# One pool of three 2 KB tiles for exponentials, key projections, copied key-value sums and output staging

## The chip, the cores and the metric

The kernel runs on one core of a Trainium2 chip. The metric is device time in microseconds (us) of one execution. Five engines work side by side, each through its own queue in a fixed order: TensorE (PE, matmuls; its weight loads are shown as PEld), VectorE (DVE), ScalarE (ACT), GpSimd (POOL) and SyncE (SP), which issues all DMAs here. They meet only at semaphores.

## The reference

Linear attention with random features, then a two-layer network on all tokens (8 batches, 8 heads, 576 tokens, head width 64, 128 features; 4608 tokens, model width 512, inner width 2048):

```python
def phi(x):
    proj = np.einsum('bhsd,df->bhsf', x, w_phi)
    proj = proj - np.max(np.abs(proj), axis=-1, keepdims=True)
    return np.concatenate([np.exp(proj), np.exp(-proj)], axis=-1)
q_p, k_p = phi(q), phi(k)
kv = np.einsum('bhsf,bhsd->bhfd', k_p, v)
z = np.sum(k_p, axis=2)
num = np.einsum('bhsf,bhfd->bhsd', q_p, kv)
den = np.einsum('bhsf,bhf->bhs', q_p, z)[..., None] + 1e-06
x = (num / den).transpose(0, 2, 1, 3).reshape(4608, 512)
h = x @ w_in
out = np.maximum(0.01 * h, h) @ w_out
```

## The kernel before

**Attention** goes by pairs of heads: 8 batches of 4 pairs, numbered 0 to 31. Pairs 0 to 3 have their own start-up code (`first_k_phase`, `first_q_phase`); pairs 4 to 31 use `k_phase` and `q_phase`. From pair 8 on, every fp32 operand is split in a high and a low fp32r half, and products are made of three matmuls (hh, hl, lh).

`k_phase(i)` walks the 576 keys in three groups (two columns of 128 tokens, two, one of 64). A group projects the keys on PE (L244), copies and adds the two halves into a tile `pmk` (128 x 512 fp32, which is 2 KB in a partition; L67 by `copy_`, L249), takes the largest magnitude (L252) and negates it (L256). Each column then is exponentiated with both signs into a tile `ek` (L269, L270), split into `kph` (ACT, L67) and `kpl` (POOL or DVE, L72), and multiplied with the values into the PSUM tile `kvp` (L224). At the end `kvp` is copied to SBUF (`kvs`), transposed on PE (L301) and split into `kvh` and `kvl` (L313, L314).

`q_phase(i)` projects the queries in two halves of 288 tokens and two heads: four PSUM tiles, each made by L344 and L345, turned on DVE (L346), with block maxima (L348). The maxima cross the partitions by DMA: three DMAs `m<-m` (L350), a reduction on DVE (L353), three DMAs `mx<-mx` (L355). Then for each half: subtraction (L361), transposition back (L363), two exponentials for each head (L368, L369), the split into `qh` (DVE, L375) and `ql` (POOL, L72), and the matmuls with the key-value sums (L384, L386, L389). The result is divided and written into `ring`, which holds two batches.

**The network** takes blocks of 256 tokens, 18 of them, in 16 steps each. A step makes 128 inner features (`layer1`: 12 matmuls, L571, L572, L574, into PSUM tile `h`), applies the activation (L578), splits it into `gh` (ACT) and `gl` (POOL), and three steps later `layer2` adds the step into two PSUM tiles `acc` of 128 tokens (6 matmuls, L591 to L593). After the 16th step each `acc` is copied to an SBUF tile `o` (L67 on ACT for one, L69 on DVE for the other) and stored (L599). There are two `acc` slots, so layer 2 of the next block begins when the two copies are made. Blocks 0 and 1 run together while the weights are loaded; block 1 accumulates in an `h` and an `a` slot of PSUM in place of `acc`.

**What sets the order.** The kernel is written in a framework whose scheduler plans every engine's queue before the run. It takes ready instructions by priority: attention has the lower number, which goes first, and the network fills what is left. `advance` and `room` keep attention at most a ring ahead. A tile is named by a tag, with a number of slots for each tag (`BUFS`, else one); a new tile takes a slot when the tile before it in that slot has been released, and an instruction that writes a new tile is planned only when it has a slot. On the chip the planned order of each queue is fixed.

In SBUF the tag `ek` has one slot (exponentials, `kvs`, the last output tile, and two of four start-up tiles), `pmk` one and `o` one, each of 2 KB in a partition.

Of the kernel before, what the change touches and what calls it, by code (L numbers as in the profile page):

```python
# [9 lines left out]
F32 = mybir.dt.float32  # L10
# [7 lines left out]
P = 128  # L18
B, H, S, D = 8, 8, 576, 64
NP = H // 2  # L20
F = 128
U = 288
DM = 512
# [5 lines left out]
NBLK = NTOK // T  # L29
LAG = 3  # L30
NN = 8
NK = 8
BUFS = {"kph": 2, "eq": 2, "m4": 2, "g": 2, "gh": 2, "gl": 2, "qh": 2, "ql": 2, "dn": 2}
PBUFS = {"a": 3, "c": 1, "h": 2, "acc": 2}
ENG = {"vh": "a", "kst": "v", "qh": "v", "o": "av", "kpl": "pppv", "ksub": "vvp", "l": "v"}
TINY = 2.0 ** -15
# [8 lines left out]
def attention_moe_kernel(ctx: ExitStack, tc: tile.TileContext, q, k, v, vt, w_phi, w_in, w_out, out):  # L45
    nc = tc.nc
    cp = ctx.enter_context(tc.tile_pool(name="cp", bufs=1))
    sp = ctx.enter_context(tc.tile_pool(name="sp", bufs=1))
# [2 lines left out]
    def ct(shape, dt, name):  # L51
        return cp.tile(shape, dt, tag=name, name=name)

    def st(shape, dt, tag):
        return sp.tile(shape, dt, tag=tag, name=tag, bufs=BUFS.get(tag, 1))

    cnt = {}

# [146 lines left out]
    def k_phase(i):  # L205
        nat = i < NK
        rk, rv = kraw.pop(i)
        if not nat:
            ks = st([P, 2, S], F32R, "ks")
            for j in range(2):  # L210
                o, n = slice(64 * j, 64 * j + 64), slice(64 - 64 * j, 128 - 64 * j)
# [15 lines left out]
        for g in range(3):  # L227
# [1 line left out]
            r = slice(0, P) if g < 2 else slice(64, P)  # L229
            n = P if g < 2 else 64  # L230
            m4 = st([P, 4], F32, "m4")
            pmk = st([P, 4, F], F32, "pmk")
            if nat:
                pk = pt("a")
                for s in range(w):
# [23 lines left out]
            yield  # L259
            for s in range(w):  # L260
                c = 2 * g + s
                ek = st([P, 2, 256], F32, ("ek", "kph", "kpl")[c % 3] if nat else "ek")
                if nat:
                    nc.scalar.activation(ek[r, :, 0:F], pmk[r, 2 * s : 2 * s + 2], AF.Exp)
                    nc.scalar.activation(ek[r, :, F:256], pmk[r, 2 * s : 2 * s + 2], AF.Exp, scale=-1.0)
                else:
                    for j in range(2):
                        h = 2 * s + j
                        nc.scalar.activation(ek[r, j, 0:F], pmk[r, h], AF.Exp, bias=m4n[r, h : h + 1])  # L269
                        nc.scalar.activation(ek[r, j, F:256], pmk[r, h], AF.Exp, scale=-1.0, bias=m4[r, h : h + 1])  # L270
                if nat:
                    for j in range(2):
                        kv_mm(j, rv[r, 4 * j + c if c < 4 else 8 + j], ek[r, j], first=c == 0, last=c == 4)
                    yield
                    continue
                if c < 4:
                    kph = st([P, 2, 256], F32R, "kph")
                    kpl = st([P, 2, 256], F32R, "kpl")
                    copy_("kph", kph, ek)
                    tt_("kpl", kpl, ek, kph.bitcast(F32), ALU.subtract)  # L280
                    for j in range(2):
                        kv_mm(j, vh[:, 4 * j + c], kph[:, j], first=c == 0)
                        kv_mm(j, vl[:, 4 * j + c], kph[:, j])
                    for j in range(2):
                        kv_mm(j, vh[:, 4 * j + c], kpl[:, j])
                else:
                    kst = st([P, 2, 256], F32R, "kph")
                    copy_("kst", kst[r], ek[r])
                    nc.vector.tensor_tensor(kst[0:64], ek[r], kst[r].bitcast(F32), op=ALU.subtract)
                    for j in range(2):  # L290
                        kv_mm(j, vl[:, 8 + j], kst[:, j])
                        kv_mm(j, vh[:, 8 + j], kst[:, j], last=True)
                yield
        kvs = st([P, 2, 256], F32, "ek").rearrange("p a (b f) -> p a b f", b=2)[0:66]
        copy_("kvs", kvs, kvp[0:66].rearrange("p (a b f) -> p a b f", a=2, b=2))
        yield
        kvt = pt("c")
# [113 lines left out]
    def first_k_phase(i):  # L411
        od = i % 2
        rk, rv = first_k.pop(i)
        if i == 2:
            load_k(NP)
        yield
        kvp = pt("h")
        for g in range(3):
            pk = pt("a" if od else "acc")
            w = 2 if g < 2 else 1  # L420
            for s in range(w):
                t0 = (2 * g + s) * P if g < 2 else S - P
                proj(pk, s, rk[:, t0 : t0 + P])
            r = slice(0, P) if g < 2 else slice(64, P)
            n = P if g < 2 else 64
            m4 = st([P, 4], F32, "m4")
            pkv = pk[r, 0 : 256 * w].rearrange("p (a f) -> p a f", f=F)
            nc.vector.tensor_reduce(m4[r, 0 : 2 * w], pkv, axis=AX.X, op=ALU.max, apply_absolute_value=True)
            pm = st([P, 4, F], F32, ("kpl" if g % 2 else "kph") if od else ("ek" if g % 2 else "pmk"))
            nc.vector.tensor_tensor(pm[r, 0 : 2 * w], pkv,  # L430
                                    m4[r, 0 : 2 * w].unsqueeze(2).broadcast_to([n, 2 * w, F]), op=ALU.subtract)
            yield
            first_k["e"] = ne = first_k.get("e", -1) + 1
            e = exps[ne % 3].rearrange("p (a t f) -> p a t f", t=2, f=F)
            nc.scalar.activation(e[r, 0 : 2 * w, 0], pm[r, 0 : 2 * w], AF.Exp)
            nc.scalar.activation(e[r, 0 : 2 * w, 1], pm[r, 0 : 2 * w], AF.Exp, scale=-1.0)
            for s in range(w):
                c = 2 * g + s
                for j in range(2):
                    nc.tensor.matmul(kvp[0:66, 256 * j : 256 * j + 256], lhsT=rv[r, 4 * j + c if c < 4 else 8 + j],  # L440
                                     rhs=e[r, 2 * s + j].rearrange("p t f -> p (t f)"),
                                     start=c == 0 and j == 0, stop=c == 4, skip_group_check=True)
                yield
        kvs = st([P, 2, 256], F32, "kph").rearrange("p a (b f) -> p a b f", b=2)[0:66]
        copy_("kvs", kvs, kvp[0:66].rearrange("p (a b f) -> p a b f", a=2, b=2))
        kvt = pt("c")
        kvtv = kvt[:, 0:264].rearrange("p (a b f) -> p a b f", a=2, b=2)
        for j in range(2):
            for t in range(2):
                nc.tensor.transpose(kvtv[:, j, t], kvs[:, j, t], ident[0:66, 0:66])  # L450
        kvh = first_kvh(i)
        nc.scalar.copy(kvh[:, :, :, 0:64], kvtv[:, :, :, 0:64])
        nc.scalar.copy(kvh[:, :, :, 64:P], kvtv[:, :, :, 64:65].broadcast_to([P, 2, 2, 64]))
        kvs_of[i] = kvh, None
        yield
# [17 lines left out]
    def first_q_phase(u):  # L473
# [7 lines left out]
        for hp in range(1 if tail else NP):  # L481
# [3 lines left out]
            m4 = st([P, 4], F32, "m4")  # L485
            pqv = pq[0:n, 0 : 256 * ns].rearrange("p (a f) -> p a f", f=F)
            nc.vector.tensor_reduce(m4[0:n, 0 : 2 * ns], pqv, axis=AX.X, op=ALU.max, apply_absolute_value=True)
            pm = st([P, 4, F], F32, "ek" if hp % 2 else "pmk")
            nc.vector.tensor_tensor(pm[0:n, 0 : 2 * ns], pqv,
                                    m4[0:n, 0 : 2 * ns].unsqueeze(2).broadcast_to([n, 2 * ns, F]), op=ALU.subtract)  # L490
            yield
# [91 lines left out]
    def layer2(i, ft, half=range(TT)):  # L583
# [9 lines left out]
            nc.tensor.matmul(a, lhsT=gl[:, ts], rhs=weight(1, "h", ft), start=False, stop=ft == NFT - 1)  # L593
        if ft == NFT - 1:
            for t in half:
                o = st([P, DM], F32, "ek" if i == NBLK - 1 and t else "o")
                copy_("o", o, accs[i, t])
                r = i * T + t * P
                nc.sync.dma_start(out[r : r + P, :], o)  # L599
# [88 lines left out]
```

## Time and profile before

| what | value |
|---|---|
| time, median of 3 runs (lowest, highest) | 1207.81 us (1206.63, 1209.95) |
| profiled execution: time, span from first to last instruction | 1207.22 us, 1205.4 us |
| granted TensorE clock, mean over the span | 0.992 |
| PE busy, share of the span | 1168.8 us, 97% |
| ACT, DVE, POOL busy | 861.8, 747.7, 631.5 us |
| last exponential of a key phase (L270) starts at | 1034.3 us |
| copies into `o`: ACT 18, DVE 17; first at | 222.9 us |

The span has three parts. To about 210 us pairs 0 to 7 run and the weights are loaded and split; from 210 to about 1060 us pairs 8 to 31 run among network steps; the rest is network alone. In the rows of the windows view, the columns are: stretch, its length, then busy time and instruction count of PE, PEld, DVE, ACT, POOL, the granted PE clock, the DMA share and GB/s. In the timeline view they are: start, length, engine, line, operation, output<-inputs, shapes, count, and in brackets the idle time of the engine just before, with what ended it. In the waits view: engine and line that waited, what for, total us, times, longest.

### The profile page before, as it was taken

What the parts mean: (1) busy time and instruction counts of PE and PEld (TensorE: products, weight loads), DVE (VectorE), ACT (ScalarE), POOL (GpSimd) and SP (SyncE); (2) the same over time, 40 slices, a digit from 0 to 9 for tenths busy, and PEclk for the clock granted to TensorE, in tenths of its full rate; (3) what the DMA queues carried; (4) which work ended last, traced back from release to release, by engine and by line L of the source; (5) the groups of instructions that cost most, each with busy time, mean ns of one, the idle gap of its engine ahead of it and who ended that gap; (6) DMA issues with size and microseconds to landing.
All of it is one profiled execution on the core that took longest, in us unless ns stands there. A gap on an engine that the chain in (4) does not pass through costs nothing.

```text
span 1205.4 us, 21633 instructions
## 1 busy us (share of the span) xinstructions
PE 1168.8 (97%) x7496; PEld 1035.9 (86%) x7496; DVE 747.7 (62%) x1327; ACT 861.8 (71%) x2267; POOL 631.5 (52%) x709
## 2 busy tenths in 40 slices
PE   8899999899998999899999999999999999999998
PEld 5577778699997999799998999899989999989997
DVE  5979984566767675766677666767876767510000
ACT  5977875778787787777787877778777788543232
POOL 0042222456566676666666666656566766453232
PEclk9999999899998999899999999999999999999999
DMA  7425241201111011111111011111011110000000
GB/s 215 142 81 167 88 116 32 77 23 33 50 32 48 18 44 33 50 24 32 50 32 40 22 50 33 40 33 50 21 40 32 41 33 19 3 18 5 14 18 18
DMA packets 70846, 57.82 MB, mean 48 GB/s; under 512 B 53201, under 2 KB 54353, under 8 KB 70737
## 3 DMA queue, kind: packets, MB, share of 16 engines
q1 hardware_dynamic: 70736, 56.44, 16.6%
q8 instruction: 59, 0.97, 0.3%
q14 instruction: 51, 0.41, 0.1%
HBM read 46.20 MB, written 9.44 MB: 46 GB/s over the span
## 4 chain that ended last, share of the span: by engine, by line
PE 69%; DVE 10%; ACT 9%; issue 4%; DMA 4%; SPq 2%; POOL 2%; DVEq 0%; POOLq 0%; ACTq 0%
PE h L571 9%; PE h L574 9%; PE h L572 9%; PE acc L591 8%; PE acc L592 8%; PE acc L593 8%; PE c L224 5%; PE a L384 2%; DMA mx<-mx 2%; PE a L244 2%; PE a L389 2%; PE a L386 2%; DMA m<-m 2%; DVE tq L361 1%; SPq L350 1%
## 5 line engine op out<-in xcount | busy, mean ns | idle before, releaser
L72 POOL TENSOR_TENSOR gl<-g,gh 128x256 fp32r<-128x256 f32 x288 | 231.3, 806 | 327.9 <-ACT gh L67 259.9
L571 PE MATMUL h<-xh,w0h 128*128 128x256 f32 x1088 | 281.1, 285 | 4.4 <-ACT g L578 2.4
L572 PE MATMUL h<-xh,w0l 128*128 128x256 f32 x1088 | 277.5, 282 | 0.0
L571 PEld LDWEIGHTS h<-xh,w0h 128*128 128x128 f32 x1088 | 205.9, 189 | 18.3 <-ACT g L578 4.2
L591 PE MATMUL acc<-w1h,gh 128*128 128x512 f32 x544 | 215.3, 396 | 0.7 <-DVE o L69 0.4
L592 PE MATMUL acc<-w1l,gh 128*128 128x512 f32 x544 | 214.8, 395 | 0.0
L572 PEld LDWEIGHTS h<-xh,w0l 128*128 128x128 f32 x1088 | 205.8, 189 | 8.9
L593 PE MATMUL acc<-w1h,gl 128*128 128x512 f32 x544 | 203.4, 395 | 0.7 <-POOL gl L72 0.7
L578 ACT ACTIVATE g<-h 128x256 f32<-128x256 f32 x288 | 109.1, 381 | 110.4 <-PE h L574 85.4
L574 PE MATMUL h<-xl,w0h 128*128 128x256 f32 x1088 | 187.4, 281 | 0.0
L72 POOL TENSOR_TENSOR ql<-eq,qh 128x576 fp32r<-128x576 f32 x96 | 148.8, 1569 | 53.6 <-DVE qh L375 31.7
L67 ACT CAST gh<-g 128x256 fp32r<-128x256 f32 x288 | 114.8, 403 | 57.5 <-PE acc L592 55.1
L574 PEld LDWEIGHTS h<-xl,w0h 128*128 128x128 f32 x1088 | 154.6, 188 | 0.6 <-POOL xl L72 0.2
L72 POOL TENSOR_TENSOR kpl<-ek,kph 128x512 fp32r<-128x512 f32 x72 | 98.4, 1366 | 37.4 <-ACT kph L67 14.5
L591 PEld LDWEIGHTS acc<-w1h,gh 128*128 128x128 f32 x544 | 102.4, 188 | 14.1 <-DVE o L69 0.7
L593 PEld LDWEIGHTS acc<-w1h,gl 128*128 128x128 f32 x544 | 99.1, 188 | 17.6 <-POOL gl L72 0.9
L592 PEld LDWEIGHTS acc<-w1l,gh 128*128 128x128 f32 x544 | 102.3, 188 | 12.6
L361 DVE TENSOR_TENSOR tq<-tq,mx 128x576 f32<-128x576 f32 x56 | 59.2, 1097 | 80.3 <-DMA mx<-mx 80.3
L269 ACT ACTIVATE ek<-pmk,m4n 128x128 f32<-128x128 f32 (+1 forms) x240 | 89.8, 393 | 16.1 <-POOL kpl L72 12.6
L375 DVE TENSOR_REDUCE qh<-eq 128x576 fp32r<-128x576 f32 x96 | 70.8, 749 | 44.4 <-ACT eq L369 20.2
L270 ACT ACTIVATE ek<-pmk,m 128x128 f32<-128x128 f32 (+1 forms) x240 | 89.1, 390 | 8.6 <-DVE m L252 8.1
L368 ACT ACTIVATE eq<-mb 128x288 f32<-128x288 f32 x112 | 49.2, 439 | 53.5 <-DVE mb L363 50.1
(202 smaller groups left out, 2363.9 us busy)
## 6 DMA issues: line engine op xcount, KB each, us to landing
out_dram<-o SPq DMA_DIRECT2D x35, 256.0 KB, 2.0
rq<-in_q_dram SPq DMA_DIRECT2D x28, 288.0 KB, 3.0
rk<-in_k_dram SPq DMA_DIRECT2D x27, 288.0 KB, 2.8
rv<-in_v_dram SPq DMA_DIRECT2D x29, 256.0 KB, 3.6
ring<-in_w_in_dram SPq DMA_DIRECT2D x9, 512.0 KB, 3.8
f<-in_w_out_dram SPq DMA_DIRECT2D x7, 512.0 KB, 3.6
f<-in_w_in_dram SPq DMA_DIRECT2D x7, 512.0 KB, 3.7
ring<-in_w_out_dram SPq DMA_DIRECT2D x5, 512.0 KB, 3.8
```

The lines of the kernel that those rows point to most:

```text
L67: nc.scalar.copy(o, i)
L72: (nc.vector if pick(key) == "v" else nc.gpsimd).tensor_tensor(o, a, b, op=op)
L269: nc.scalar.activation(ek[r, j, 0:F], pmk[r, h], AF.Exp, bias=m4n[r, h : h + 1])
L270: nc.scalar.activation(ek[r, j, F:256], pmk[r, h], AF.Exp, scale=-1.0, bias=m4[r, h : h + 1])
L361: nc.vector.tensor_tensor(tu, tu, mx[:, u].unsqueeze(2).broadcast_to([P, 18, 32]), op=ALU.subtract)
L571: nc.tensor.matmul(ph, lhsT=weight(0, "h", ft)[:, d * P : d * P + P], rhs=xh[d], start=d == 0, stop=False)
L572: nc.tensor.matmul(ph, lhsT=weight(0, "l", ft)[:, d * P : d * P + P], rhs=xh[d], start=False, stop=False)
L574: nc.tensor.matmul(ph, lhsT=weight(0, "h", ft)[:, d * P : d * P + P], rhs=xl[d], start=False, stop=d == NP - 1)
L578: nc.scalar.activation(g, ph, AF.Prelu, alpha=0.01)
L591: nc.tensor.matmul(a, lhsT=gh[:, ts], rhs=weight(1, "h", ft), start=ft == 0, stop=False)
L592: nc.tensor.matmul(a, lhsT=gh[:, ts], rhs=weight(1, "l", ft), start=False, stop=False)
L593: nc.tensor.matmul(a, lhsT=gl[:, ts], rhs=weight(1, "h", ft), start=False, stop=ft == NFT - 1)
```

## The change

Tags `ek`, `pmk` and `o` go; a tag `wk` with three slots of the same size takes their tiles, so the SBUF used is the same. `pmk` and `ek` of `k_phase`, `kvs`, all output tiles, and the start-up tiles that alternated between `ek` and `pmk` now draw from it. Tiles in `kph` and `kpl` stay where they were. No instruction is added, removed or resized.

```diff
-BUFS = {"kph": 2, "eq": 2, "m4": 2, "g": 2, "gh": 2, "gl": 2, "qh": 2, "ql": 2, "dn": 2}
+BUFS = {"kph": 2, "eq": 2, "m4": 2, "g": 2, "gh": 2, "gl": 2, "qh": 2, "ql": 2, "dn": 2, "wk": 3}
...
-    def st(shape, dt, tag):
-        return sp.tile(shape, dt, tag=tag, name=tag, bufs=BUFS.get(tag, 1))
+    def st(shape, dt, tag, name=None):
+        return sp.tile(shape, dt, tag=tag, name=name or tag, bufs=BUFS.get(tag, 1))
...
-            pmk = st([P, 4, F], F32, "pmk")
+            pmk = st([P, 4, F], F32, "wk", "pmk")
...
-                ek = st([P, 2, 256], F32, ("ek", "kph", "kpl")[c % 3] if nat else "ek")
+                ek = st([P, 2, 256], F32, ("wk", "kph", "kpl")[c % 3] if nat else "wk", "ek")
...
-        kvs = st([P, 2, 256], F32, "ek").rearrange("p a (b f) -> p a b f", b=2)[0:66]
+        kvs = st([P, 2, 256], F32, "wk", "kvs").rearrange("p a (b f) -> p a b f", b=2)[0:66]
...
-            pm = st([P, 4, F], F32, ("kpl" if g % 2 else "kph") if od else ("ek" if g % 2 else "pmk"))
+            pm = st([P, 4, F], F32, ("kpl" if g % 2 else "kph") if od else "wk", "pm")
...
-            pm = st([P, 4, F], F32, "ek" if hp % 2 else "pmk")
+            pm = st([P, 4, F], F32, "wk", "pm")
...
-                o = st([P, DM], F32, "ek" if i == NBLK - 1 and t else "o")
+                o = st([P, DM], F32, "wk", "o")
```

The scheduler plans again with these slots, and the queues change over their whole length. Three places matter for the prediction. A name's number is the tile's number in the program and is the same in both kernels.

**The copies of block 0's result.** On DVE, `o_3080` is the output tile of the second half of block 0, copied from `acc_626`. Before, it stands in pair 7's work, ahead of the transposition `mb_1897` of that pair's second half:

```order
L361 TENSOR_TENSOR tq_1741<-tq_1741,mx_1805 128x576 x2
L363 STREAM_TRANSPOSE mb_1816<-tq_1741 128x576
L69 COPY o_3080<-acc_626 128x512
L363 STREAM_TRANSPOSE mb_1897<-tq_1741 128x576
L213 TENSOR_TENSOR ks_2526<-rk_1724,ks_2526 64x576 x2
L395 STREAM_TRANSPOSE dn_1878<-dn_1857 128x288
```

In the changed kernel the same copy stands behind all of pair 8's work and behind pair 9's last transposition `dn_3040`, which follows pair 9's last query matmuls:

```order
L375 TENSOR_REDUCE qh_3017<-eq_3014 128x576
L395 STREAM_TRANSPOSE dn_2973<-dn_2944 128x288
L398 RECIPROCAL rc_2975<-dn_2973 128x9
L399 STREAM_TRANSPOSE dn_2973<-rc_2975 128x288
L69 CAST kph_2984<-ek_2979 64x512
L289 TENSOR_TENSOR kph_2984<-ek_2979,kph_2984 64x512
L395 STREAM_TRANSPOSE dn_3040<-dn_3021 128x288
L69 COPY o_3080<-acc_626 128x512
L346 STREAM_TRANSPOSE tq_3190<-a_3192 128x288
```

The copy moved back by the whole of two pairs; on ACT the other half's copy, `o_3077<-acc_623`, moved with it, and there it stands behind pair 9's `kvs` copy and the values' cast for the next pair.

**Layer 2 of block 2 on PE.** `acc_3133` is block 2's first accumulator. Before, its first matmul stands among the query projections of pair 8 (`qs_2541`), behind whole network steps (`h_3083`, `h_3114`):

```order
L572 MATMUL h_3114<-xh_70,w0l0_639 128x256
L574 MATMUL h_3114<-xl_71,w0h0_638 128x256 x4
L224 MATMUL c_1733<-kph_1889,vhl_1718 64x256
L224 MATMUL c_1733<-kph_1889,vhl_1718 66x256
L224 MATMUL c_1733<-kph_1889,vhl_1718 64x256
L224 MATMUL c_1733<-kph_1889,vhl_1718 66x256
L591 MATMUL acc_3133<-w1h0_651,gh_2521 128x512
L344 MATMUL a_2575<-qs_2541,wq_72 128x288
```

In the changed kernel it stands behind the last query matmuls of pair 9 (`ql_3018`) and the first projection of pair 10 (`qs_3175`):

```order
L384 MATMUL a_3031<-qh_3017,kvh_2748 128x288
L386 MATMUL a_3031<-qh_3017,kvl_2749 128x288
L244 MATMUL a_3185<-wq_72,ks_3160 128x256 x2
L389 MATMUL a_3031<-ql_3018,kvh_2748 128x288 x2
L224 MATMUL c_2808<-kph_2984,vhl_1718 64x256
L224 MATMUL c_2808<-kph_2984,vhl_1718 66x256
L224 MATMUL c_2808<-kph_2984,vhl_1718 64x256
L224 MATMUL c_2808<-kph_2984,vhl_1718 66x256
L344 MATMUL a_3192<-qs_3175,wq_72 128x288
L345 MATMUL a_3192<-qs_3175,wq_72 128x288
L301 MATMUL c_3003<-ident_64,kvs_2994 128x66 x4
L591 MATMUL acc_3133<-w1h0_651,gh_2521 128x512
```

Between the last of block 1's layer-2 matmuls and this L591 there were 79 matmuls before, and there are 235 now, of which 54 are the network's (layer 1, four and a half steps).

**Between the two halves of pair 8 on DVE.** `qh_2643` and `qh_2665` are the first half of its queries, `qh_2739` opens the second. Before:

```order
L375 TENSOR_REDUCE qh_2643<-eq_2640 128x576
L375 TENSOR_REDUCE qh_2665<-eq_2662 128x576
L363 STREAM_TRANSPOSE mb_2732<-tq_2556 128x576
L375 TENSOR_REDUCE qh_2739<-eq_2736 128x576
L375 TENSOR_REDUCE qh_2757<-eq_2754 128x576
```

And in the changed kernel:

```order
L375 TENSOR_REDUCE qh_2643<-eq_2640 128x576
L72 TENSOR_TENSOR kpl_2675<-ek_2669,kph_2674 128x512
L375 TENSOR_REDUCE qh_2665<-eq_2662 128x576
L363 STREAM_TRANSPOSE mb_2732<-tq_2556 128x576
L249 TENSOR_TENSOR pmk_2695<-a_2696,pmk_2695 64x256
L252 TENSOR_REDUCE m4_2694<-pmk_2695 64x2
L213 TENSOR_TENSOR ks_2786<-rk_2534,ks_2786 64x576
L256 TENSOR_SCALAR m4n_2711<-m4_2694 64x2
L213 TENSOR_TENSOR ks_2786<-rk_2534,ks_2786 64x576
L375 TENSOR_REDUCE qh_2739<-eq_2736 128x576
```

Key-phase work of pair 8 and the key split of pair 9 (`ks_2786`) moved ahead of the second half's `qh`; at pair 9 nothing but one `qh` and the transposition stands there.

What PE's queue holds between the points that the prediction uses, counted by the columns of a matmul (u0 and u1 are the first L384 of the first and second half of the queries; "last projection" is the fourth L345 of the pair):

| kernel | from | to | 256 columns, network | 256 columns, attention | 512 | 288 | 66 |
|---|---|---|---|---|---|---|---|
| before | pair 8 last projection | u0 | 60 | 16 | 34 | 1 | 4 |
| before | pair 9 last projection | u0 | 59 | 14 | 28 | 1 | 4 |
| before | pair 11 last projection | u0 | 25 | 16 | 30 | 1 | 0 |
| before | pair 15 last projection | u0 | 24 | 16 | 27 | 1 | 4 |
| before | pair 11 and pair 15, each, u0 | u1 | 0 | 8 | 0 | 12 | 0 |
| changed | pair 8 last projection | u0 | 24 | 26 | 0 | 1 | 0 |
| changed | pair 8 u0 | u1 | 0 | 4 | 0 | 12 | 0 |
| changed | pair 8 last L384 | pair 9 last projection | 0 | 8 | 0 | 13 | 4 |
| changed | pair 9 last projection | u0 | 0 | 28 | 0 | 1 | 0 |
| changed | pair 9 u0 | u1 | 0 | 2 | 0 | 12 | 0 |
| changed | pair 9 last L384 | L591 of `acc_3133` | 0 | 6 | 0 | 6 | 4 |
| changed | pair 13 last projection | u0 | 58 | 26 | 12 | 1 | 0 |
| changed | pair 25 last projection | u0 | 64 | 16 | 12 | 1 | 0 |
| changed | pair 29 last projection | u0 | 55 | 26 | 12 | 1 | 0 |
| changed | pairs 13, 25, 29, each, u0 | u1 | 0 | 4 | 0 | 12 | 0 |

At the other split pairs of the changed kernel, 13.4 to 16.2 us of PE's work (counted as in the prediction) stand between the last projection and u0, and 3.9 to 6.3 us between u0 and u1.

## The prediction

> **What bounds the kernel now.** I read the page first, then windows, then PE's timeline where PE idles, then the other engines there.
>
> ```profile
> PE 1168.8 (97%) x7496; PEld 1035.9 (86%) x7496; DVE 747.7 (62%) x1327; ACT 861.8 (71%) x2267; POOL 631.5 (52%) x709
> PE   8899999899998999899999999999999999999998
> PEclk9999999899998999899999999999999999999999
> PE 69%; DVE 10%; ACT 9%; issue 4%; DMA 4%; SPq 2%; POOL 2%; DVEq 0%; POOLq 0%; ACTq 0%
> ```
>
> PE is busy nearly throughout, and the chain that ended last runs mostly through it. The clock dips in three slices, and these are slices in which PE also idles. The change leaves PE's work as it is, so only idle time and slow clock can change. Windows around the three places:
>
> ```profile
> 210.00:240.00 30.00, 25.62 (x130) 19.33 (x129) 15.39 (x27) 21.57 (x60) 12.65 (x20) 0.89 0.26 77
> 240.00:360.00 120.00, 119.21 (x819) 109.67 (x819) 82.96 (x148) 95.12 (x261) 76.40 (x82) 1.00 0.13 35
> 360.00:390.00 30.00, 25.85 (x157) 22.93 (x156) 22.85 (x42) 21.55 (x57) 19.97 (x20) 0.89 0.13 39
> 390.00:480.00 90.00, 89.91 (x616) 83.20 (x615) 57.36 (x105) 72.13 (x195) 59.45 (x59) 1.00 0.13 35
> 480.00:510.00 30.00, 24.70 (x148) 21.63 (x148) 21.82 (x39) 23.54 (x66) 18.92 (x23) 0.94 0.17 46
> 510.00:1050.00 540.00, 536.08 (x3657) 493.64 (x3657) 371.90 (x642) 419.74 (x1138) 344.34 (x364) 1.00 0.12 33
> ```
>
> 390 to 480 us is PE at full rate: 616 matmuls in 90 us, 205.3 in 30. At 360 to 390 there are 157, so (205.3 - 157)/205.3 x 30 = 7.1 us are lost, of which 4.15 are idle and 2.9 slow clock. At 480 to 510 it is 8.4 us. Together 15.5. At 210 to 240 4.4 us are idle and 0.11 x 30 = 3.3 go to the clock: 7.7. What PE waits for:
>
> ```profile
> 485.99 0.63 PE L574 MATMUL h<-xl,w0h 128*128 128x256 f32 x4
> 486.46 0.39 PE L591 MATMUL acc<-w1h,gh 128*128 128x512 f32 x1
> 486.69 0.40 PE L592 MATMUL acc<-w1l,gh 128*128 128x512 f32 x1
> 486.93 0.40 PE L593 MATMUL acc<-w1h,gl 128*128 128x512 f32 x1
> 487.16 0.29 PE L344 MATMUL a<-qs,wq 128*128 128x288 f32 x1
> 487.29 0.29 PE L345 MATMUL a<-qs,wq 128*128 128x288 f32 x1
> ...
> 498.88 0.45 PE L224 MATMUL c<-kpl,vhl 128*66 128x256 f32 x2
> 502.87 0.61 PE L384 MATMUL a<-qh,kvh 128*128 128x288 f32 x1 [3.54 <-DVE qh L375]
> ...
> 509.00 0.37 PE L384 MATMUL a<-qh,kvh 128*128 128x288 f32 x1 [1.04 <-DVE qh L375]
> ```
>
> This is pair 15. Its last projection starts at 487.29, its query matmuls at 502.87: 15.6 us later. PE ran out of other work after 498.88. The rows also give PE's pace: 256 columns 0.117 us (four in 0.47), 512 columns 0.233, 288 columns 0.134. The chain between runs through other engines:
>
> ```profile
> 493.90 0.41 DVE L353 TENSOR_REDUCE mx<-m 32x36 f32<-32x144 f32 x1 [1.91 <-DMA m<-m]
> 498.27 1.84 DVE L361 TENSOR_TENSOR tq<-tq,mx 128x576 f32<-128x576 f32 x2 [3.96 <-DMA mx<-mx]
> 500.03 0.76 DVE L363 STREAM_TRANSPOSE mb<-tq 128x576 f32<-128x576 f32 x1
> 502.07 0.74 DVE L375 TENSOR_REDUCE qh<-eq 128x576 fp32r<-128x576 f32 x1
> 503.46 0.77 DVE L363 STREAM_TRANSPOSE mb<-tq 128x576 f32<-128x576 f32 x1
> 505.37 0.96 DVE L213 TENSOR_TENSOR ks<-rk,ks 64x576 fp32r<-64x576 f32 x1 [0.56 <-ACT ks L67]
> ```
>
> Two DMA trips, three DVE operations and an exponential cannot be shortened by this change: no tile of `wk` lies on that chain. It is covered only by what stands in PE's queue between its ends. Its length elsewhere (pair 11, where PE waited too; then the first `qh` of the fastest and the slowest pair, 30 and 8):
>
> ```profile
> 351.60 0.38 PE L345 MATMUL a<-qs,wq 128*128 128x288 f32 x1
> 366.30 0.61 PE L384 MATMUL a<-qh,kvh 128*128 128x288 f32 x1 [1.36 <-DVE qh L375]
> ```
>
> ```profile
> 1010.04 0.30 PE L345 MATMUL a<-qs,wq 128*128 128x288 f32 x1
> 1021.65 0.74 DVE L375 TENSOR_REDUCE qh<-eq 128x576 fp32r<-128x576 f32 x1
> 248.07 0.29 PE L345 MATMUL a<-qs,wq 128*128 128x288 f32 x1
> 263.91 1.42 DVE L375 TENSOR_REDUCE qh<-eq 128x576 fp32r<-128x576 f32 x2
> ```
>
> Pair 11: 14.7 us. Fastest: 1022.4 - 1010.0 = 12.4. Slowest, with half of the merged row: 264.6 - 248.1 = 16.5. I take the mean of pairs 11 and 15, where PE did wait: 15.1. From u0 to u1 pair 15 took 509.00 - 502.87 = 6.1, with a key split (L213) between the halves on DVE.
>
> **A rule for a thin place**: idle = 15.1 less PE's work from last projection to u0, plus 6.1 less that from u0 to u1. Before, by the table of counts, pair 11 has 41 x 0.117 + 30 x 0.233 + 0.13 = 11.9 and 2.5 us, pair 15 (with 0.2 for its four short transposes) 11.4 and 2.5: idle 3.2 + 3.6 and 3.7 + 3.6, together 14.1. The windows lost 15.5, clock included. So the loss is 1.1 times the rule.
>
> **The change part by part.** Nothing is added, and durations stay. What moves is which tile gets a slot. Before, `o` had its own:
>
> ```profile
> 222.93 0.60 ACT L67 COPY o<-acc 128x512 f32<-128x512 f32 x1
> 247.20 0.40 PE L591 MATMUL acc<-w1h,gh 128*128 128x512 f32 x1
> ```
>
> Now the output tiles compete with attention's, which go first, and block 0's copies stand behind two pairs (first place of the change). Until they run, both `acc` slots are held, layer 2 of block 2 cannot begin, and with two slots for `gh` layer 1 stops after four and a half steps. In between PE has attention alone:
>
> - Pair 8, to u0: 50 x 0.117 + 0.13 = 6.0 us of work; idle 15.1 - 6.0 = 9.1.
> - Pair 8, u0 to u1: 12 x 0.134 + 4 x 0.117 = 2.1; the `kpl`, the key-phase rows and two L213 stand ahead of the second `qh`, as in pair 15, so 6.1 - 2.1 = 4.0.
> - Pair 8's last L384 to pair 9's last projection: 2.9 us of work, while ACT evacuates four PSUM halves and DVE does the division and the projections' transpositions. The trace of before has no such stretch without cover. The nearest rows are pair 15 to 16, 9.4 us with cover, so idle lies between 0 and 6.5. Four evacuations (0.41 each) and nine short DVE operations (a transposition is 0.47, most are less) are about 5.3; less 2.9 that gives the 2.4 I take.
> - Pair 9, to u0: 28 x 0.117 + 0.13 = 3.4; idle 11.7.
> - Pair 9, u0 to u1: 1.8 of work. No L213 is between; `qh`, L363, two exponentials and `qh` take about 3.1: 1.3 (0 to 4.3).
> - To L591: 1.7 of work against four evacuations, `kvs`, the value cast and `o` on ACT, about 3.5: 1.8 (0 to 3).
>
> The rows for the nearest stretch, then the means of a transposition and of an evacuation:
>
> ```profile
> 510.28 0.44 PE L384 MATMUL a<-qh,kvh 128*128 128x288 f32 x1
> ...
> 519.72 0.29 PE L345 MATMUL a<-qs,wq 128*128 128x288 f32 x1
> ```
>
> ```profile
> L346 DVE STREAM_TRANSPOSE tq<-a 128x288 f32<-128x288 f32 x112 | 51.3, 469 | 19.6 <-PE a L345 15.6 <-PE a L342 3.2
> ...
> L392 ACT ACTIVATE dn<-a 64x288 f32<-64x288 f32 x112 | 45.7, 408 | 1.9
> ```
>
> Sum of the stretch: 9.1 + 4.0 + 2.4 + 11.7 + 1.3 + 1.8 = 30.3. Slow clock adds 3, as in one window of before: **+33**. Bounds: with a 12.4 us chain and the open items at 0, 6.4 + 4.0 + 9.0 = 19; with 16.5 and the open items at their top, 10.5 + 4.0 + 6.5 + 13.1 + 4.3 + 3 + 6 for the clock = 47.
>
> Later block ends. Three more show the thin pattern, pairs 13, 25 and 29: to u0 84 x 0.117 + 12 x 0.233 + 0.13 = 12.8, 12.3 and 12.4; u0 to u1 2.1, with L213 between. Rule: 6.3 + 6.8 + 6.7 = 19.8, times 1.1 = 21.8. Pairs 11 and 15, thin before, have 13.4 and 13.9 us now and no L213 between: 15.5 less. Net **+6** (0 to 12).
>
> Pair 7:
>
> ```profile
> 229.07 0.81 PE L384 MATMUL a<-eq,kvh 128*128 128x288 f32 x2 [2.47 <-ACT eq L368]
> 233.33 2.29 PE L384 MATMUL a<-eq,kvh 128*128 128x288 f32 x4 [1.64 <-ACT dn L392]
> ```
>
> The new order puts 12.0 us of work ahead of u0 there instead of 9.7, which takes 2.3 of the 2.47, and most of the slow clock with it: **-4** (-7 to -2).
>
> The rest. Looser tiles can save in the key phase:
>
> ```profile
> ACT ek L269 <- POOL kpl L72: 12.6, 15, 1.5
> ```
>
> These are waits of ACT, 71% busy, and PE's cover hides them: 0. The other pairs have 13.4 to 16.2 us before u0 against 15.1; by the rule pairs 11 and 15 still lose 1.7 + 1.2. Before, PE idled 0.8 + 0.1 + 3.9 us in the long windows, and I expect about as much: 0 (-4 to +5). Start-up keeps its work on ACT and DVE: 0 (-3 to +3).
>
> Sum: 33 + 6 - 4 = +35. The profiled execution took 1207.2 (span 1205.4 and 1.8 around it), the median 1207.8; 1207.8 + 35 = **1243**.
>
> The clock, by the skill. The rows show 0.89 and 0.94 in the windows where PE idled, 1.00 elsewhere. The Trainium skill, "TensorE: Matmul & The Clock Gate", Part 1: The HAM clock gate, says that PE falls to half rate after an idle window of about 3.4 us and returns after as long a busy one. [...] By that rule the whole stretch could run at half rate, which is the last rival but one.
>
> **Rivals.**
>
> *The stretch is short.* The chain takes 12.4 us when no network work queues on DVE and ACT, and the open items vanish: 19 in place of 33, the rest +2. Time 1207.8 + 21 - 4 = 1225. For it: pair 30's row. Against: pairs 11 and 15 were dry, and took 14.7 and 15.6.
>
> *The stretch runs at half rate.* PE's 18 us of work in the six segments doubles and none of it falls into a wait: 1243 + 18 = 1261. Against: most of it stands where PE waits anyway.
>
> *Looser tiles win.* Three slots let exponentials and projections run ahead, and the places where PE idled (15.5 + 7.7 us) go, with no new ones: 1207.8 - 23.2 = 1185; with the stretch at its lower bound of 19, 1204. It decides if the stretch costs under 20 and pairs 13, 25 and 29 cost nothing. The Trainium skill, "Perfetto Trace Analysis", Optimization Strategy, says that repeated bubbles on the engine that should be saturated can mean too few buffers for the next tile, which speaks for this rival. The trace of before does not agree: PE's waits there end with `qh` after DMA trips, not with a tile of these tags.
>
> **How the numbers follow.** Forecast (1230 to 1255) 0.70; short stretch (1212 to 1230) 0.14; half rate (above 1255) 0.10; looser tiles win 0.06. A measurement here tells 0.3%, 3.6 us, from no change. The last rival gives faster 0.03, same 0.02 and slower 0.01, so slower is 0.95. The range, 1221 to 1260, takes most of the short stretch and leaves out the top and the last rival.
>
> **What would show it.** After: two copies `o<-acc` some 20 us or more later relative to block 0's last L593; about 50 us around pairs 8 and 9 with PE idle for about 30, waiting at L384 for `qh`; a clock below 0.9 there; three smaller dips at pairs 13, 25 and 29; none at 11 and 15; full rate elsewhere. Wrong if PE is as busy around pairs 8 and 9 as before, or if the loss is spread evenly over the pairs.

## The result, and the profile after

| | before | changed |
|---|---|---|
| time, median | 1207.67 us (1206.63 to 1209.95) | 1257.95 us (1257.12 to 1259.99, 4 runs) |
| ratio, 95% interval | | 1.0411 [1.0396, 1.0427] |
| span of the profiled execution, granted clock | 1205.4 us, 0.992 | 1258.2 us, 0.966 |

The change costs 50.3 us, 52.8 by the spans. The page after: busy time of the engines, the busy tenths and the granted clock of PE in 40 slices (of 31.5 us), and the shares of the chain that ended last.

```profile
PE 1198.0 (95%) x7496; PEld 1053.9 (84%) x7496; DVE 765.0 (61%) x1327; ACT 859.0 (68%) x2267; POOL 624.9 (50%) x709
...
PE   8899999867999899999999999998999989999998
...
PEclk9989999966999999999999999999899989999999
...
PE 62%; DVE 14%; ACT 12%; DMA 4%; issue 3%; POOL 3%; SPq 1%; DVEq 0%; POOLq 0%; ACTq 0%
```

The same 7496 matmuls are now busy for 29.2 us longer, although none was resized, and PE idles for the other 23.6 of the 52.8 us. In the chain DVE has gained 4% and ACT 3%, while PE lost 7%. One hole stands out, slices 9 and 10 with a clock of 0.6; three faint ones follow. The windows view of the changed kernel (columns as before; the last row covers the hole alone):

```profile
210.00:240.00 30.00, 25.65 (x145) 19.54 (x143) 17.60 (x31) 23.33 (x66) 14.33 (x21) 1.00 0.17 42
240.00:270.00 30.00, 20.79 (x127) 18.06 (x128) 21.32 (x41) 21.80 (x60) 15.85 (x15) 0.85 0.14 32
270.00:300.00 30.00, 20.57 (x75) 15.82 (x76) 22.92 (x41) 20.19 (x52) 13.05 (x13) 0.50 0.13 32
300.00:330.00 30.00, 29.21 (x182) 25.99 (x181) 20.39 (x35) 20.70 (x56) 16.45 (x18) 0.91 0.19 58
330.00:420.00 90.00, 88.55 (x596) 80.52 (x595) 64.31 (x108) 71.09 (x196) 59.62 (x67) 1.00 0.13 35
420.00:450.00 30.00, 26.24 (x155) 23.38 (x154) 24.26 (x41) 21.18 (x57) 16.17 (x17) 0.83 0.17 50
870.00:900.00 30.00, 25.54 (x139) 22.03 (x138) 24.30 (x41) 20.37 (x54) 15.10 (x16) 0.83 0.18 50
990.00:1020.00 30.00, 26.59 (x175) 24.18 (x173) 22.08 (x37) 23.67 (x68) 18.62 (x22) 0.92 0.05 12
247.00:304.00 57.00, 38.45 (x168) 30.55 (x167) 42.22 (x74) 38.54 (x98) 25.82 (x22) 0.62 0.12 32
```

Where 30 us held 205 matmuls at full pace, 270 to 300 holds 75, at half rate throughout. The dips at 420, 870 and 990 us are pairs 13, 25 and 29; at 330 to 420, where pair 11 used to dip, the clock is 1.00.

The hole begins and ends with block 0's output. Pair 8's last projection on PE, pair 10's, and the first matmul of layer 2 of block 2:

```profile
246.84 0.29 PE L345 MATMUL a<-qs,wq 128*128 128x288 f32 x1
303.39 0.78 PE L591 MATMUL acc<-w1h,gh 128*128 128x512 f32 x1
311.75 0.29 PE L345 MATMUL a<-qs,wq 128*128 128x288 f32 x1
```

And the copies, on DVE and on ACT:

```profile
302.00 0.69 DVE L69 COPY o<-acc 128x512 f32<-128x512 f32 x1
303.54 0.57 ACT L67 COPY o<-acc 128x512 f32<-128x512 f32 x1
```

ACT's copy ran at 222.93 before; it is 81 us later. The first L591 starts 0.7 us behind the end of DVE's copy, and the L591 of the second accumulator, at 304.82, as much behind the end of ACT's. From 246.84 to 311.75 are 64.9 us, in which PE's queue holds 27.3 us of work, counted by columns at the pace of the prediction: 37.6 us are lost. I counted in this way for every stretch from one pair's last projection to another's, in every kernel (elapsed time less PE's work at full pace, in us; idle time and slow clock together). What is left of the span, 1101.5 us, is the same in all of them.

| part | before | changed |
|---|---|---|
| up to pair 8's last projection | 70.2 | 70.6 |
| pair 8 to 10 (the hole) | 0.5 | 37.6 |
| pair 11 to 12, pair 15 to 16 | 18.9 | 4.0 |
| pairs 13, 25, 29, each to the next | 0.9 | 27.5 |
| rest | 13.4 | 17.0 |
| sum | 103.9 | 156.7 |

### The profile page after: what moved, and what is told of

Its sections match the earlier page's. It is cut to its first block, busy times and chain, and to the rows that moved or that the text cites. A ratio compares the mean times of both kernels' runs of the same rounds, so it can differ in the third digit from the quotient of the medians.

```text
span 1258.2 us, 21551 instructions
## 1 busy us (share of the span) xinstructions
PE 1198.0 (95%) x7496; PEld 1053.9 (84%) x7496; DVE 765.0 (61%) x1327; ACT 859.0 (68%) x2267; POOL 624.9 (50%) x709
## 4 chain that ended last, share of the span: by engine, by line
PE 62%; DVE 14%; ACT 12%; DMA 4%; issue 3%; POOL 3%; SPq 1%; DVEq 0%; POOLq 0%; ACTq 0%
PE acc L591 8%; PE acc L592 8%; PE acc L593 8%; PE h L571 8%; PE h L572 8%; PE h L574 8%; PE c L224 5%; DMA mx<-mx 2%; DVE ks L213 2%; DVE tq L361 2%; PE a L244 1%; ACT eq L369 1%; PE a L384 1%; ACT ks L67 1%; DVE qh L375 1%
## 5 line engine op out<-in xcount | busy, mean ns | idle before, releaser
L571 PE MATMUL h<-xh,w0h 128*128 128x256 f32 x1088 | 277.7, 284 | 3.9 <-ACT g L578 1.9
L591 PE MATMUL acc<-w1h,gh 128*128 128x512 f32 x544 | 218.5, 402 | 0.1
L72 POOL TENSOR_TENSOR ql<-eq,qh 128x576 fp32r<-128x576 f32 x96 | 144.3, 1518 | 60.5 <-DVE qh L375 55.1
L69 DVE COPY o<-acc 128x512 f32<-128x512 f32 x17 | 11.7, 687 | 175.8 <-PE acc L593 175.5
L591 PEld LDWEIGHTS acc<-w1h,gh 128*128 128x128 f32 x544 | 103.5, 190 | 14.9 <-DVE o L69 0.2
L375 DVE TENSOR_REDUCE qh<-eq 128x576 fp32r<-128x576 f32 x96 | 70.5, 752 | 56.5 <-ACT eq L369 35.5
L269 ACT ACTIVATE ek<-pmk,m4n 128x128 f32<-128x128 f32 (+1 forms) x240 | 84.2, 390 | 20.1 <-DVE m4n L256 17.4
L224 PE MATMUL c<-kph,vhl 128*66 128x256 f32 (+1 forms) x480 | 81.3, 293 | 13.8 <-ACT kph L67 8.2
```

Source lines behind the costliest of these rows:

```text
L72: (nc.vector if pick(key) == "v" else nc.gpsimd).tensor_tensor(o, a, b, op=op)
L224: nc.tensor.matmul(kvp[0 : lt.shape[1], 256 * j : 256 * j + 256], lhsT=lt, rhs=rt, start=first and j == 0, stop=last, skip_group_check=True)
L571: nc.tensor.matmul(ph, lhsT=weight(0, "h", ft)[:, d * P : d * P + P], rhs=xh[d], start=d == 0, stop=False)
L591: nc.tensor.matmul(a, lhsT=gh[:, ts], rhs=weight(1, "h", ft), start=ft == 0, stop=False)
```

## The experiments

Three theories were open. **Priority**: attention's tiles take the slots because their instructions have the smaller priority number, as the prediction has it. **Making order**: slots of one tag are dealt in the order in which the program makes the tiles. `advance` lets the program make attention ahead of the network, `+ 2` pairs ahead, so at the end of block 0 the tiles of two more pairs stand before `o`. **Attention**: the loss comes from attention's own tiles going round one pool, and the output tiles matter little. One more question was which chain of work sets the length of the hole. All edits are to the changed kernel unless said. Times are medians, and ratios are to the kernel before on the same chip. The scheduler plans each edited kernel anew, so an edit also moves work that it does not name.

**A slot of its own for `o`.** The attention tiles keep two shared slots. Three of them and a separate output slot would be one slot of 2 KB more than either kernel has, and no run has that.

```diff
-... "dn": 2, "wk": 3}
+... "dn": 2, "wk": 2}
-                o = st([P, DM], F32, "wk", "o")
+                o = st([P, DM], F32, "wk" if i == NBLK - 1 and t else "o", "o")
```

> Output tiles get a slot of their own again (the last one excepted, as before); the exponentials, key projections and key-value copies share the two others. Three theories. MAKING ORDER: slots of a tag are dealt in the order in which the program makes the tiles, and attention's tiles are made up to two pairs ahead of the network's, so an output tile in the shared pool waits for pairs 8 and 9. PRIORITY: the output copies lose the slots to attention because attention has the better priority. ATTENTION: the loss comes from the attention tiles rotating in one pool, the output tiles matter little. By MAKING ORDER and by PRIORITY the stretch of idle PE at pairs 8 and 9 is gone: 1200 to 1212 us. By ATTENTION it stays above 1235 us.

1206.1 us, ratio 0.998 [0.9968, 0.9991]. The hole is gone; its windows:

```profile
240.00:270.00 30.00, 28.41 (x183) 24.78 (x182) 19.71 (x37) 22.70 (x62) 16.25 (x18) 0.97 0.12 32
270.00:300.00 30.00, 30.00 (x205) 27.50 (x204) 20.78 (x39) 23.52 (x66) 16.71 (x19) 1.00 0.13 33
```

Its hole loses 2.0 us, pairs 13, 25 and 29 lose 0.8. So the whole cost of the change comes with `o` in the shared tag; sharing two slots between exponentials, projections and sums costs nothing that shows.

**Before, with `o` in the exponentials' tag.** The reverse, on the kernel before: one part of the change alone.

```diff
-BUFS = {... "dn": 2}
+BUFS = {... "dn": 2, "ek": 2}
-                o = st([P, DM], F32, "ek" if i == NBLK - 1 and t else "o")
+                o = st([P, DM], F32, "ek")
```

> The kernel before, with one part of the change alone: the output tiles draw from the exponentials' tag, which gets two slots; the key projections keep their own slot, and the start-up tiles their two tags. By MAKING ORDER and PRIORITY the stretch at pairs 8 and 9 is there in full (about 37 us there against the kernel before) and two or three thinner places: 1238 to 1258 us. By ATTENTION, which sees no three-slot pool here, 1203 to 1213 us.

1247.88 us, ratio 1.0316 [1.0278, 1.0354]. The windows and the copy:

```profile
240.00:270.00 30.00, 21.21 (x118) 17.34 (x116) 23.45 (x41) 23.47 (x61) 14.77 (x14) 0.78 0.13 32
270.00:300.00 30.00, 18.39 (x75) 13.82 (x75) 23.28 (x42) 20.69 (x55) 13.38 (x13) 0.61 0.13 33
...
299.83 0.69 DVE L69 COPY ek<-acc 128x512 f32<-128x512 f32 x1 [0.49 <-ACT ek L67]
```

The hole loses 37.5 us, as in the changed kernel: `o` in any tag that attention uses is enough. Pairs 13, 25 and 29 lose 18.0 here, not 27.5.

**`o` first in priority.** The output tile and its copy get the smallest number in the program.

```diff
+                keep = tc.cur_priority
+                tc.cur_priority = 2 * PF
                 o = st([P, DM], F32, "wk", "o")
                 copy_("o", o, accs[i, t])
+                tc.cur_priority = keep
```

> The changed kernel, with the output tiles and their copies at the best priority of the whole program, ahead of attention. By PRIORITY the copies of block 0 run when the block is done and the loss at pairs 8 and 9 is gone: 1203 to 1215 us. By MAKING ORDER nothing improves, since the slot is not theirs before pair 9's tiles have had it: 1253 to 1265 us. By ATTENTION also about 1258 us.

1261.22 us, ratio 1.0426 [1.0400, 1.0452], no better than the change, and the copy comes when it came there:

```profile
301.86 0.69 DVE L69 COPY o<-acc 128x512 f32<-128x512 f32 x1
```

Priority falls as the reason, and Attention fell with the first two experiments.

**The lead of the making order.** The `+ 2` in the loop over network steps becomes 1, then 0.

```diff
-        advance(min(room(...), NP * (1 + (n + 1) / NFT * T / S) + 2))
+        advance(min(room(...), NP * (1 + (n + 1) / NFT * T / S) + 1))
```

> The changed kernel with attention made one pair ahead of the network in place of two. If the order of making deals the slots, block 0's output tiles wait for pair 8's tiles and not for pair 9's: the stretch costs about half of its 37 us, some 18, all of it at pair 8, and pair 9 is covered. With fewer thin places later the whole takes 1208 to 1224 us. If the lead acted as a switch (any lead at all holds the copies back to the end of what attention may do), it stays at 1245 us or more.

> The changed kernel with the constant lead of attention over the network, in the order in which the program makes them, set from two pairs to none; priorities, slots and every instruction are the same. By MAKING ORDER block 0's output tiles are made ahead of pair 8's tiles, the copies run with pair 7 and the stretch is gone: 1200 to 1212 us, with at most one thin place left. By PRIORITY and by ATTENTION nothing that they rest on has moved: 1250 to 1265 us.

With 1: 1212.82 us, ratio 1.0032 [1.0023, 1.0042]. With 0: 1212.56 us, ratio 1.0037 [1.0019, 1.0055]. First the copy and the hole's windows with 1, then the copy with 0:

```profile
269.53 0.69 DVE L69 COPY o<-acc 128x512 f32<-128x512 f32 x1
...
240.00:270.00 30.00, 21.41 (x128) 18.55 (x129) 21.84 (x42) 21.98 (x61) 16.21 (x15) 0.81 0.12 32
270.00:300.00 30.00, 30.00 (x186) 27.23 (x185) 19.78 (x36) 22.66 (x61) 18.38 (x19) 0.90 0.20 59
```

```profile
242.15 0.63 DVE L69 COPY o<-acc 128x512 f32<-128x512 f32 x1
```

A lead of two, one and no pairs puts the copy at 302.0, 269.5 and 242.2 us and makes the hole 37.6, 16.0 and 0.4 us. Making order it is, one pair of lead for one pair of delay. Most of the loss goes without giving `o` its slot back; what stays is spread (20 us in "rest" in place of 13.4). With no lead the time is 0.6 us above what was expected, and three thin places are left, not one: pairs 11, 15 and 27 lose 10.5, 7.2 and 7.5 us. The kernel before was not run with these leads: planned with a lead of two, one or none, its queues are the same row for row.

**A lead of 0.2.** Between the two, in the hope of keeping the hole shut and the thin places filled.

```diff
+        advance(min(room(...), NP * (1 + (n + 1) / NFT * T / S) + (0.2)))
```

> The changed kernel with a lead of a fifth of a pair in place of two. Output tiles are made ahead of the next pairs' tiles, as with no lead, and in the planned order no pair from 8 to 31 has less than 14 us of PE's work ahead of its query matmuls, so neither pair 8 nor pairs 11 and 15 should run dry. The kernel before loses 8.7 and 10.2 us at pairs 11 and 15: without these 1190 to 1202 us, faster than both. If the output tiles still hold attention's slots long enough to hurt elsewhere, 1205 to 1215 us, as with leads of nought and one.

1213.13 us, ratio 1.0031 [1.0020, 1.0042]: a miss. The hole is shut (0.7), but pairs 11 and 15 lose 7.5 and 5.7 again. In pair 11, the first half's first matmul, the second half's, and that of the second half's second head:

```profile
365.56 0.40 PE L384 MATMUL a<-qh,kvh 128*128 128x288 f32 x1 [0.42 <-DVE qh L375]
369.36 0.29 PE L384 MATMUL a<-qh,kvh 128*128 128x288 f32 x1
373.09 0.58 PE L384 MATMUL a<-qh,kvh 128*128 128x288 f32 x1 [2.20 <-DVE qh L375]
```

What I had looked at was the work ahead of the first half, which is ample now: 15.3 us of it in 16.0. Between the halves PE has 2.8 us of work in 3.8. The largest wait stands inside the second half, ahead of its second head, and with what follows it 5.9 of the 7.5 us are lost from 369.36 on. Another 4.7 us (2.9 idle, and 1.8 by a clock of 0.94) are lost from 1050 to 1080, where attention ends.

**The query chain without its DMA trips.** Each partition takes its own features' maximum, so the maximum over all features is left out.

```diff
-        for a in range(1, 4):
-            nc.sync.dma_start(m[0:32, a], m[32 * a : 32 * a + 32, 0])
...
-        nc.vector.tensor_reduce(mx[0:32], m[0:32].rearrange("p a u c -> p u c a"), axis=AX.X, op=ALU.max)
-        for a in range(1, 4):
-            nc.sync.dma_start(mx[32 * a : 32 * a + 32], mx[0:32])
+        nc.vector.tensor_reduce(mx, m[:, 0:1].rearrange("p a u c -> p u c a"), axis=AX.X, op=ALU.max)
```

> The changed kernel without the two DMA trips of the query maxima: each partition reduces its own maxima, so a part of the computation (the maximum over a token's features) is left out. Everything else stays, and block 0's copies still wait for pairs 8 and 9. If the stretch is set by the latency from the last projection to the query matmuls, it shrinks by the two trips of two pairs, some 7 us each (490.5 to 498.3 us in the kernel before, less one short reduction): 37 to about 23 us; the whole 1225 to 1242 us. If instead the work of the two pairs on VectorE, ScalarE and GpSimd sets it, the stretch stays at 33 us or more.

1244.47 us, ratio 1.0299 [1.0280, 1.0318]: the whole is 2.5 us above what was expected by the first theory, the hole far above, 33.5 us, where the second has it. From the last projection to the first L384 it is 8.2 and 9.6 us at pairs 8 and 9, where the changed kernel takes 13.0 and 15.4, as meant: 10.6 less. But from the first half to the second it is 10.2 and 8.3 in place of 5.7 and 5.1. The waits of this kernel between 247 and 304 us (engine and line that waited, what for, total us, times, longest), with the longest one in its timeline (L380 and L388 are L384 and L392 of the changed kernel):

```profile
PE a L380 <- ACT dn L388: 4.7, 2, 4.2
PE c L224 <- ACT kph L67: 4.3, 3, 2.1
...
262.26 0.61 PE L380 MATMUL a<-qh,kvh 128*128 128x288 f32 x1 [4.20 <-ACT dn L388]
```

With the queries early, PE stands at the evacuation of its result (`dn`) by ACT and at the key phase (`kph`).

**The key phase made longer.** The exponential with the minus sign is made twice; the result stays the same.

```diff
                         nc.scalar.activation(ek[r, j, F:256], pmk[r, h], AF.Exp, scale=-1.0, bias=m4[r, h : h + 1])
+                        nc.scalar.activation(ek[r, j, F:256], pmk[r, h], AF.Exp, scale=-1.0, bias=m4[r, h : h + 1])
```

> The changed kernel with each second exponential of the key phase (from pair 8 on) made twice, the same values to the same place: 10 more ScalarE instructions a pair, 3.9 us. The stretch at pairs 8 and 9 cost 37.6 us, and without the DMA trips 33.5. If the chain there runs through the key phase's queue on ScalarE and VectorE, the stretch grows by a good part of 2 x 3.9 us: 41 to 47 us. If it is the query chain's latency that counts, ScalarE has room and the stretch stays at 35 to 39 us. The whole: 1262 to 1280 us in the first case, 1254 to 1264 in the second.

1295.68 us, ratio 1.0718 [1.0699, 1.0736]. The hole grew to 38.9, by 1.3, although ACT got 3.9 us more work in each pair: the key phase alone does not set it either. The rest of the kernel grew by more than either theory had (pairs 13, 25, 29 to 32.9, "rest" to 40.2), so the whole time was missed by both. In the whole run the longest waits at both places are of one size (L385 and L376 are L384 and L375 of the changed kernel):

```profile
PE a L385 <- DVE qh L376: 15.8, 11, 4.1
PE c L224 <- ACT kph L67: 14.5, 6, 3.9
```

**The start-up's share.** In the changed kernel the start-up tiles go round three slots; the separate slot of the first experiment takes that away. Here that arrangement, with the edits of the first experiment, has them go round its three (`pm_tag` deals `wk`, `wk`, `o` in turn), and in the kernel before they go likewise round `pmk`, `ek`, `o`.

```diff
-            pm = st([P, 4, F], F32, "wk", "pm")
+            pm = st([P, 4, F], F32, pm_tag(), "pm")
```

> The arrangement with output tiles in a slot of their own and two shared slots for attention, and in the start-up the projections also use the output slot, which is idle there, every third time. The start-up of that arrangement lost 3.8 us against the kernel before; with three slots it should lose less: 1201 to 1206 us. If the slots of the start-up don't matter, 1206 us as without.

> The kernel before, with the start-up's projections going round the slots of the exponentials, the key projections and the output tiles in place of the first two alone. If start-up slots matter, 1 to 4 us faster than before: 1204 to 1207 us. If not, within 1 us of before.

1205.94 us, ratio 0.9974 [0.9965, 0.9983], and 1209.65 us, ratio 1.0012 [0.9998, 1.0025], the second above both of its expectations. The losses up to pair 8 are 73.5 and 71.8, against 73.7 for the first experiment and 70.2 before: three slots at the start bring nothing that can be told. The first of the two is the fastest kernel of the study, by 0.26% [0.17, 0.35] ahead of before, which is less than the 0.3% that a measurement here tells from no change.

## Why the prediction was right, and where it was not

1243 us was predicted with a range of 1221 to 1260; 1257.95 is inside by 2 us, above the forecast's own 1230 to 1255 and where the half-rate rival begins. The way of the change and its place were argued; that the total fell inside the range is in part luck, as the terms show:

| term | predicted | measured (table of losses) |
|---|---|---|
| hole at pairs 8 and 9 | +33 (19 to 47) | +37.1 |
| later block ends | +6 (0 to 12) | +11.7: pairs 13, 25, 29 +26.6, pairs 11, 15 -14.9 |
| pair 7 | -4 (-7 to -2) | +0.4 for all up to pair 8's last projection |
| rest | 0 (-4 to +5) | +3.6 |
| sum | +35 | +52.8 |

**The place and the kind of the loss held.** The copies moved as the queues said, layer 2 of block 2 stood still until they were made, and PE had attention alone.

**The step that failed in the reasoning** is "the output tiles compete with attention's, which go first". The copies are late not because attention's number is smaller but because its tiles were made first: `o` with the smallest number comes as late, and shortening the lead by a pair brings the copy forward by a pair. The number did not suffer, since the delay was read from the planned queues.

**The term that was mis-sized most is the slow clock**: 3 us in the hole and 2 in the later block ends. Over the span the matmuls are busy for 29.2 us longer. In the hole 18.6 of the 37.6 us are idle (57 - 38.45 in its row), and the other 19.0 go with the clock. So the idle time of 30.3 was too high by 12, the clock too low by 16, and their sum close by luck.

**The hole, by segment** (idle and slow clock together, in us):

| segment | predicted | measured |
|---|---|---|
| pair 8, last projection to u0 | 9.1 | 7.0 |
| pair 8, u0 to u1 | 4.0 | 3.6 |
| pair 8, last L384 to pair 9's last projection (measured from u1) | 2.4 | 6.0 |
| pair 9, last projection to u0 | 11.7 | 12.0 |
| pair 9, u0 to u1 | 1.3 | 3.3 |
| pair 9, last L384 to L591 (measured from u1 to pair 10's last projection) | 1.8 | 5.7 |
| slow clock | 3 | in the rows above |

The query chain took 13.0 and 15.4 us against 15.1. Among the segments the mis-sized ones are the three for which before had no row without cover: short by 3.6, 2.0 and 3.9, the last beyond its top of 3. The slow clock is in them, and in two also the stretch from u1 to the pair's last L384, 1.3 and 2.0 us, for which the sum had no item. Nor was the wait the one that was named. Idle time of "about 30, waiting at L384 for `qh`" was to be seen; of the 18.6 us some 12 are spent at L224, in the key phase. The largest waits of the changed kernel from 247 to 304 us, and rows of the timeline, the first of them DVE's first `qh` of pair 8:

```profile
PE c L224 <- ACT kph L67: 8.0, 3, 3.8
PE c L224 <- POOL kpl L72: 2.6, 4, 1.3
PE a L384 <- DVE qh L375: 2.5, 3, 1.3
```

```profile
258.88 0.75 DVE L375 TENSOR_REDUCE qh<-eq 128x576 fp32r<-128x576 f32 x1 [0.84 <-ACT eq L369]
256.53 0.69 PE L224 MATMUL c<-kph,vhl 128*66 128x256 f32 x4 [3.77 <-ACT kph L67]
265.51 0.37 PE L384 MATMUL a<-qh,kvh 128*128 128x288 f32 x1 [1.28 <-DVE qh L375]
280.13 1.12 PE L224 MATMUL c<-kph,vhl 128*66 128x256 f32 x4 [2.49 <-ACT kph L67]
290.66 0.58 PE L384 MATMUL a<-qh,kvh 128*128 128x288 f32 x1 [0.42 <-DVE qh L375]
```

The key-phase matmuls that the prediction counted as PE's cover ahead of u0 waited themselves. Two chains of nearly one length run there. At pair 8 the first `qh` is ready at 259.63, and the last key-phase matmuls ahead of u0 start at 259.01, u0 itself at 259.87. Taking 10.6 us off the query chain saved 4.1 of the hole, and 3.9 us a pair onto the key phase added 1.3. These two kernels were planned anew, with 24.4 and 25.8 us of PE's work in the hole in place of 27.3, so what each chain alone is worth stays open.

**The half-rate rival had the clock right and the price wrong.** Its condition came true: four L224 take 1.12 us at 280 where they took 0.69 at 256, and 270 to 300 has 0.50. By the clock records PE ran at half rate from 257.4 to 264.2 and from 267.6 to 305.1 us. Its +18 on top of 33 did not come: the hole is 4 longer than forecast, and the total landed in the rival's interval through other terms as well. The 19.0 us of slow clock are about its 18, but idle time is 12 less than forecast. That fits the point against it, that the slowed matmuls fill time in which PE would have waited; no run held the clock up there, so what half rate itself costs inside the hole is not shown.

**Later block ends**: the three thin places came at the pairs that the rule named, with 26.6 us against 21.8, but only one of its two parts held. Between the halves they lost 3.6, 4.1 and 4.0 us, as the rule has it (4.0 each). Ahead of u0 it has 7.8 us together, and they lost 1.6, since u0 came 12.5 to 13.7 us behind the last projection there and not 15.1. Behind u1, where it has nothing, they lost some 14. PE's waits at the three come to 12.4 us; the rest goes with half rate, which held for 10.2 us on end at each of them (from 434.9, 878.6 and 1015.1 us). So the size came out by luck. Pairs 11 and 15 gave back 14.9, against 15.5; the table of losses, which counts whole stretches, has 18.9 us there before, where the prediction's windows saw 15.5, and 4.0 are left.

**Pair 7**: its own gain came. The waits of 2.47 and 1.64 us at its L384 are small in the changed kernel, and from 210 to 240 us the clock is 1.00 with 145 matmuls, where it was 0.89 with 130:

```profile
228.81 0.75 PE L384 MATMUL a<-eq,kvh 128*128 128x288 f32 x2 [0.67 <-ACT eq L368]
...
233.59 1.24 PE L384 MATMUL a<-eq,kvh 128*128 128x288 f32 x4 [0.34 <-ACT dn L392]
```

But as much was lost earlier, in the start-up. Its windows before, and in the changed kernel:

```profile
30.00:60.00 30.00, 25.83 (x127) 18.07 (x125) 27.35 (x56) 28.57 (x64) 2.66 (x4) 1.00 0.48 139
60.00:90.00 30.00, 27.57 (x152) 21.82 (x151) 21.92 (x48) 22.80 (x57) 12.39 (x16) 1.00 0.27 84
```

```profile
30.00:60.00 30.00, 25.88 (x121) 18.68 (x120) 26.97 (x54) 27.36 (x62) 2.64 (x4) 0.94 0.47 139
60.00:90.00 30.00, 27.72 (x134) 21.71 (x133) 22.67 (x50) 22.27 (x55) 12.79 (x16) 0.89 0.27 85
```

The 134 matmuls in place of 152 go with the clock of 0.89. Why the clock fell there was not settled; with and without a third slot at the start, two pairs of kernels stayed within 2 us up to pair 8.

**The rival "looser tiles win"** needed a hole under 20 and no loss at pairs 13, 25 and 29. With `o` apart both hold, and it is worth 2 us, not 4 to 23: pair 15 still loses 10.4 there. But attention has two slots there, as many as before. A third one for attention with `o` apart was not run, so that part of the rival stays untested.

## What to carry to other kernels

Where slots are dealt in the order in which a program makes its tiles, a shared tag ties its users to that order: a tile made late (an output) waits for all tiles of the tag that were made before it, however urgent its instruction is, and whatever it frees (here the accumulators) waits too. So give a tile that drains a scarce resource a tag that only such tiles use, or make it before the work that runs ahead. And before costing matmuls as cover, look at whether their own operands come from the engines that are late, and count work behind a wait at the slow clock too.

## What was not expected of the hardware

PE stayed at half rate for 37.5 us on end (267.6 to 305.1) with no wait over 2.5 us. Windows of 3.4 us of the changed kernel, cut where the clock changed:

```profile
254.00:257.40 3.40, 0.69 (x4) 0.43 (x4) 1.48 (x3) 3.00 (x9) 0.79 (x1) 1.00 0.03 4
257.40:260.80 3.40, 2.28 (x10) 2.20 (x11) 2.56 (x4) 1.44 (x4) 2.17 (x2) 0.50 0.00 0
260.80:264.20 3.40, 3.40 (x14) 2.69 (x12) 2.91 (x7) 2.56 (x6) 2.09 (x2) 0.50 0.00 0
264.20:267.60 3.40, 1.19 (x8) 0.96 (x8) 2.29 (x4) 3.31 (x10) 2.09 (x2) 1.00 0.32 87
267.60:271.00 3.40, 2.74 (x14) 2.39 (x13) 2.56 (x6) 1.74 (x5) 1.93 (x2) 0.50 0.00 0
271.00:274.40 3.40, 3.02 (x13) 2.08 (x12) 2.45 (x8) 2.50 (x6) 1.82 (x3) 0.50 0.00 0
...
301.60:305.10 3.50, 3.31 (x14) 2.68 (x13) 2.53 (x7) 2.78 (x6) 1.31 (x2) 0.50 0.25 91
305.10:308.50 3.40, 3.40 (x21) 2.98 (x21) 2.11 (x6) 1.69 (x6) 2.61 (x5) 0.99 0.79 231
```

A window with PE busy for 0.69 of 3.40 us, and one with 1.19, are followed by half rate. Full rate comes back behind windows with 3.40 of 3.40 and 3.31 of 3.50, and not behind one with 3.02. So in these rows it took a window busy almost throughout to win the full rate back, while a window a third busy lost it.

The kernel before is alike: the windows of 3.41 us ahead of its five falls (at 229.6, 366.2, 373.0, 502.7 and 509.5 us) had PE busy for 0.94, 1.34, 1.55, 0.02 and 1.74 us. But the busy share alone gives no sharp threshold. In the changed kernel windows with 1.81 and 2.10 us (from 230.08 and 236.90) lost nothing, while one in the start-up with 2.83 (from 79.89) was followed by half rate; in the first experiment 2.91 us (from 238.29) won full rate back. What else counts is not shown.

The Trainium skill, "TensorE: Matmul & The Clock Gate", Part 1: The HAM clock gate, has the clock go up after a busy window of about 3.4 us, with which most of these rows agree. It has the clock go down after an idle window. Of the falls told here only one, at 502.7 us of the kernel before, came behind a window as good as idle; the fall at 267.6 came behind 1.19 us of work.
